# Windowed attention and a softplus MLP on one core: the written-out order of all work is replaced by another one

## The chip, the core and the metric

The kernel runs on one core of a Trainium2 chip. A core has five engines that each work through their own queue of instructions in order: TensorE (PE in the profile, with PEld for its weight loads), VectorE (DVE), ScalarE (ACT), GpSimd (POOL) and SyncE (SP), which here only issues DMA transfers. POOL and ACT issue DMA transfers too. [...]

The metric is the device time of one execution in microseconds. Before the change it is 343.13 us, the median of 3 runs (340.19 to 346.43).

## The reference: what is computed

Eight batches of eight heads, 576 positions, head size 64. Each position attends to the positions within 32 of its own and to 8 global positions; the 8 global positions attend to all. The result, laid out as 4,608 tokens of 512 features, goes through two matrix products with a softplus between them.

```python
scores = scale * np.matmul(q, k.transpose(0, 1, 3, 2))
mask = np.abs(pos[:, None] - pos[None, :]) <= window      # window = 32
mask = mask | is_global[:, None] | is_global[None, :]
scores = np.where(mask, scores, -1000000000.0)
scores = scores - np.max(scores, axis=-1, keepdims=True)
attn = np.exp(scores)
attn = attn / (np.sum(attn, axis=-1, keepdims=True) + 1e-09)
attn_out = np.matmul(attn, v)
x = attn_out.transpose(0, 2, 1, 3).reshape(B * S, H * D)  # 4608 x 512
h = x @ w_in                                              # 512 x 2048
g = np.maximum(h, 0.0) + np.log1p(np.exp(-np.abs(h)))
out = g @ w_out                                           # 2048 x 512
```

## The kernel before, in words

**Tiles.** The 4,608 tokens are nine tiles of 512 (m = 0 to 8). Attention works on groups of four blocks of 32 positions, called pairs in the code, n = 0 to 35, four to a tile, because 18 blocks make a batch and the tiles run across the batches. While TensorE works on the matrix products of tile m, the other engines prepare the attention of tile m + 1 (`AHEAD`, L409).

**One pair n from 4 on**, with the names that the profile gives: TensorE forms the scores (`sc`, L1040); VectorE adds the mask in two halves (`ma`, L1044) and takes the maximum (`mx`, L1057); GpSimd or VectorE subtracts it (`sub`, L1063); ScalarE takes the exponential (`ex`, L1080); VectorE sums and inverts (`su`, L1087 and L1089); GpSimd or VectorE multiplies by the inverse (`no`, L1095, output tile `pn`); VectorE transposes (`tp`, L1104, output tile `pt`). The first four pairs have the mask added by TensorE and go in halves (`mk` L1024, `mx` L1055, `ex` L1076). When the pairs of a tile (or of a piece of tiles 0 and 1) are there, TensorE multiplies by the values (`val`, L1207), and `xev` (L696, output tile `xT`) copies the result for the MLP.

**The global rows of batch b:** `sg` (L932), `mxg` (L942), `gexp` (L949), `tpg` (L954, L956, output tile `pgt`), `ov` (L965), `odd`, `both`, `gv` (L969 to L978). `pick` and `put` (L849, L862) fetch the keys and queries of the global positions; `fill` and `gev` copy them into place.

**Loads.** SP brings q, k and v of each batch as fp32 into three staging tiles (`load_part` L490 and L494 for q and k of batches 0 and 1, `load_qk` L440 for later batches, `load_v` L445). `cast` turns them into bf16 (L691 and L693 for q, L696 for k and v) on GpSimd, VectorE or ScalarE, and `turn` transposes (L789, L793; for batches 0 and 1 by TensorE, L820). A staging tile can be loaded again only after its cast. GpSimd issues the weights: `w_in` in four parts (L1304) and `w_out` in four parts (L1308), each cast from fp32 by the transfer. Two small transfers on SP, `follow` (L727), read the last bytes of `w_in` part 1 and of `w_out` part 1, so SP's later loads stay behind those weights. A one-column copy on GpSimd (L1385, `landed`) reads the end of one part of batch 1, so that `w_out` is issued only when this part is there; before the change it is `natural(0, 1)`, the q part for positions 256 to 511.

**The MLP.** `first` (L1242) is four matmuls for one of 16 slices of 128 hidden features, `soft` (L1248) is the softplus on ScalarE, `second` (L1253) one matmul of the second product, `oev` (L696, tile `osb`) the copy out of PSUM, and a store follows on GpSimd's queue for tiles 0 to 5 and on ScalarE's afterwards (L1265).

**The order.** All this work is 1,721 jobs, numbered as they are added (`_Order.add`). `ORDER` is a tuple of one number per job: five times the job's number plus its engine (0 PE, 1 ACT, 2 DVE, 3 POOL, 4 the loads on SP). It fixes which engine does each job and the sequence on every engine. `run` (L179) walks through `ORDER`, keeps a clock of its own from the costs given at `add`, and sorts the jobs by that clock before they are written out; no job of one engine passes another. So costs, `SLOW`, `NEED` and `STARVE` make no instruction: they shape the order where one is searched for, and here, with the order given, only how the five sequences are interleaved in the program text, and how many idle matmuls `keep` (L135) puts into TensorE's planned pauses before 34 us (`fill_in`, L701, the `warm` rows).

**The shared-port flags.** Jobs marked `port` (the casts, `sub`, `no`, `gv`, and after the change `make_own`) are treated in the clock of `run` as not able to run on VectorE while GpSimd computes (L217 to L220). [...]

Of the kernel before, what the change touches and what calls it, by code (L numbers as in the profile page):

```python
# [19 lines left out]
class _Order:  # L20
# [111 lines left out]
    FILL = 0.55  # L132
    fill = None

    def keep(self, t0, t1, order):  # L135
# [8 lines left out]
        count = int((t1 - t0) * self.FILL / 220)  # L144
        key = ("warm", len(order))
        j = dict(cost={"PE": (0, 0)}, emit=lambda e: self.fill(key, count), at=t0, end=t0 + count * 220, on="PE", n=-1, deps=[])
        self.fetch = self.stall(t0, count * 220, 2 * count)[1]
# [31 lines left out]
    def run(self, free):  # L179
# [13 lines left out]
        self.mine, self.other = 0, (0, 0)  # L193
        self.fetch, self.issued = (self.ASK, self.NEED, [], 0), 0
        while ready:
# [6 lines left out]
            for j in self.picked(ready):  # L202
# [57 lines left out]
            if e == "DVE" and j["port"]:  # L260
                self.mine = t + step
            if e == "POOL" and not j["moves"]:
                self.other = t, t + step
# [19 lines left out]
def kernel(  # L283
# [10 lines left out]
    nc = tc.nc  # L294
# [414 lines left out]
    def had(*keys):  # L709
        return [T[key] for key in keys]  # L710
# [715 lines left out]
```

## Time and profile before

| | before |
|---|---|
| time, median of 3 runs | 343.13 us (340.19 to 346.43) |
| profiled execution | span 340.5 us, 12,210 instructions; no other time of this execution is given |
| PE busy | 319.2 us (94%) |
| DVE busy | 259.4 us (76%) |
| ACT busy | 230.0 us (68%) |
| POOL busy | 169.1 us (50%) |
| DMA moved | 42.74 MB |
| first matmul of the MLP | 30.17 us after the start of the span |
| last matmul of attention values (`val` of tile 8) | 306.42 to 307.92 us |

How to read it: the profile is one execution. Busy times are sums over an engine's instructions, and a row of a group gives the operation, output and input tiles, the count, then the busy time and the mean of one. A row of the waits gives engine, line, what it waited for, and then the total in us, how often, and the longest. Rows of the timeline begin with the start in us from the start of the span and the duration. Queues of the DMA: q1 is SP's, q0 is GpSimd's.

### The profile page before, as it was taken

To read this page: it belongs to the slowest core of one execution; us is meant where nothing else is said; L and a number is where in the kernel's file an instruction comes from. 1 tells how busy PE (TensorE), PEld (TensorE's weight loads), DVE (VectorE), ACT (ScalarE), POOL (GpSimd) and SP (SyncE) were. 2 spreads that over 40 slices of the span, in tenths; PEclk is the share of its full clock that TensorE was granted. 3 is DMA by queue.
4 is the path that set the end of the run, shared out by engine and by line. 5 is a ranking of instruction groups with operands and counts; after the bars stand their busy time and mean duration, and the time that the engine had idled before them with its cause. 6 is when DMAs were issued, how large, how long until landed. Compare 5 with 4: busy or idle time off the path is not lost.

```text
span 340.5 us, 12210 instructions
## 1 busy us (share of the span) xinstructions
PE 319.2 (94%) x5333; PEld 169.4 (50%) x5333; DVE 259.4 (76%) x409; ACT 230.0 (68%) x469; POOL 169.1 (50%) x155
## 2 busy tenths in 40 slices
PE   6787899988999999999799999999999989999996
PEld 3435785555555454544354445444544444445443
DVE  7598679994999799979999999799985979061000
ACT  5688789975687866489638583769466746765442
POOL 5464457863695789608375328644532431460000
PEclk9679999999999999999999999999999999999999
DMA  7999499979799999999950997008111020002003
GB/s 193 220 173 244 123 162 191 175 142 192 127 171 211 174 204 185 189 151 231 164 132 34 173 165 177 2 2 171 36 56 39 33 97 2 31 31 96 0 0 123
DMA packets 168733, 42.74 MB, mean 126 GB/s; under 512 B 153192, under 2 KB 165736, under 8 KB 168680
## 3 DMA queue, kind: packets, MB, share of 16 engines
q1 hardware_dynamic: 160664, 28.33, 47.4%
q0 software_dynamic: 6144, 10.49, 13.2%
q10 hardware_dynamic: 1872, 3.15, 2.5%
q8 instruction: 41, 0.67, 0.9%
q14 instruction: 12, 0.10, 0.1%
HBM read 36.71 MB, written 9.44 MB: 136 GB/s over the span
## 4 chain that ended last, share of the span: by engine, by line
PE 41%; DVE 23%; SPq 11%; POOL 7%; DMA 7%; issue 6%; ACT 4%; POOLq 0%; DVEq 0%; ACTq 0%
PE h L1242 19%; PE o L1253 15%; SPq L440 7%; SPq L445 4%; DMA stage<-in_q_dram 4%; DVE sm L1087 4%; PE xo L1207 3%; POOL pn L1095 3%; DVE st L1044 2%; DMA stage<-in_v_dram 2%; POOL st L1063 2%; PE s L1040 2%; DVE gm L942 2%; DVE m L1057 2%; DVE pn L1095 2%
## 5 line engine op out<-in xcount | busy, mean ns | idle before, releaser
L1253 PE MATMUL o<-wout,g 128*128 128x512 bf16 (+1 forms) x592 | 137.4, 374 | 0.0
L1242 PE MATMUL h<-xT,win 128*128 128x512 bf16 (+3 forms) x768 | 135.8, 326 | 0.4 <-DVE xT L696 0.2
L1248 ACT ACTIVATE g<-h 128x512 bf16<-128x512 f32 (+3 forms) x192 | 85.5, 501 | 44.8 <-PE h L1242 43.7
L1242 PEld LDWEIGHTS <-win 128*128 128x128 bf16 x768 | 67.3, 98 | 60.3 <-issue 1.2
L1253 PEld LDWEIGHTS <-g 128*128 128x128 bf16 x592 | 55.3, 98 | 60.7 <-ACT g L1248 1.3
L1063 POOL TENSOR_TENSOR st<-st,m 128x1024 f32<-128x1024 f32 x27 | 51.9, 1931 | 49.4 <-DVE m L1057 49.3
L1095 POOL TENSOR_TENSOR pn<-st,rs 128x1024 bf16<-128x1024 f32 (+1 forms) x29 | 51.4, 1783 | 48.5 <-DVE rs L1089 46.4
L1044 DVE TENSOR_TENSOR st<-s,mask 128x512 f32<-128x512 f32 x64 | 41.5, 676 | 12.0 <-PE s L1040 12.0
L1087 DVE TENSOR_REDUCE sm<-st 128x8 f32<-128x1024 f32 x32 | 38.3, 1197 | 8.6 <-ACT st L1080 8.6
L1057 DVE TENSOR_REDUCE m<-st 128x8 f32<-128x1024 f32 x32 | 38.4, 1207 | 0.4
L1080 ACT ACTIVATE st<-st 128x1024 f32<-128x1024 f32 x32 | 32.9, 1057 | 1.1 <-POOL st L1063 1.0
L1104 DVE STREAM_TRANSPOSE pt<-pn 128x512 int32<-128x512 int32 x36 | 24.6, 690 | 3.9 <-POOL pn L1095 3.6
L696 ACT CAST xT<-xo 128x512 bf16<-128x512 f32 (+3 forms) x31 | 12.9, 476 | 17.9 <-PE xo L1207 17.9
L696 ACT COPY osb<-o 128x512 f32<-128x512 f32 (+1 forms) x29 | 16.6, 577 | 11.1 <-PE o L1253 9.8
L1095 DVE TENSOR_TENSOR pn<-st,rs 128x1024 bf16<-128x1024 f32 (+1 forms) x11 | 19.9, 1818 | 0.1
L696 POOL CAST kb<-stage 128x1152 bf16<-128x1152 f32 (+2 forms) x12 | 14.4, 1218 | 8.1 <-DVE rs L1089 5.1
L949 ACT ACTIVATE pg<-sg,gnb 128x320 bf16<-128x320 f32 (+1 forms) x32 | 14.9, 575 | 5.0 <-DVE gnb L943 5.0
L693 POOL TENSOR_SCALAR qb<-stage 128x1152 bf16<-128x1152 f32 (+2 forms) x10 | 12.9, 1286 | 10.7 <-DMA stage<-in_v_dram 7.3
L1248 ACT ACT_TABLE_LOAD x13 | 16.7, 1283 | 0.5 <-PE h L1242 0.3
L1040 PE MATMUL s<-kx,qx 64*32 64x128 bf16 x1152 | 15.4, 224 | 1.3 <-DVE qx L789 0.6
L696 POOL CAST vb<-stage 128x1152 bf16<-128x1152 f32 x11 | 12.6, 1145 | 7.2 <-DMA stage<-in_v_dram 5.5
L1265 POOL DMA_DIRECT2D out_dram<-osb x24 | 14.0, 584 | 3.7 <-DVE osb L696 3.7
(124 smaller groups left out, 313.2 us busy)
## 6 DMA issues: line engine op xcount, KB each, us to landing
stage<-in_v_dram SPq DMA_DIRECT2D x64, 144.0 KB, 4.6
stage<-in_k_dram SPq DMA_DIRECT2D x48, 144.0 KB, 3.8
stage<-in_q_dram SPq DMA_DIRECT2D x48, 144.0 KB, 3.6
out_dram<-osb POOLq DMA_DIRECT2D x24, 256.0 KB, 3.2
out_dram<-osb ACTq DMA_DIRECT2D x11, 256.0 KB, 2.1
stage<-in_k_dram SPq DMA_DIRECT2D x4, 512.0 KB, 9.1
stage<-in_q_dram SPq DMA_DIRECT2D x4, 512.0 KB, 6.2
win<-in_moe_w_in_dram POOLq DMA_DIRECT2D x4, 512.0 KB, 6.9
```

The source lines that it names most:

```text
L440: eng.dma_start(out=stage[w][quad(r), :, e, :], in_=SRC[w][b, HG * g:HG * g + HG].rearrange("a (c i e) (f d) -> e f i (a c) d", i=BL, e=2, ...
L696: {"ACT": nc.scalar.copy, "DVE": V.tensor_copy, "POOL": nc.gpsimd.tensor_copy}[e](out, in_)
L1044: V.tensor_tensor(out=PS["st", n][:, h, :, :], in0=PS["s", n, h][:, :, :], in1=mask[:, h, j0:j0 + PB, :, :].rearrange("p j s i -> p j (s i ...
L1057: V.reduce_max(out=m[:], in_=flat(PS["st", n], h0, h1), axis=AX)
L1063: on(e).tensor_tensor(out=t, in0=t, in1=over(PS["m", n, y][:], SL * BL), op=OP.subtract)
L1080: nc.scalar.activation(out=t, in_=t, func=AF.Exp)
L1087: V.reduce_sum(out=sm[:], in_=flat(PS["st", n], h0, h1), axis=AX)
L1095: on(e).tensor_tensor(out=PS["pn", n][:, :, :, h0:h1].rearrange("p x s h -> p h x s"), in0=PS["st", n][:, h0:h1], in1=PS["rs", n, y][:].re ...
L1104: V.transpose(out=bass.AP(base.tensor, base.offset, ap=[list(base.ap[0]), [2 * STEP, PB // 2], [STEP + BL // 2, 2], [1, SL * BL]]), in_=PS ...
L1242: nc.tensor.matmul(out=h[:, :], lhsT=w_in_t[c // 4][:, kd, c % 4 * P:(c % 4 + 1) * P], rhs=PS["xT", m][:, kd, lo:hi], start=(kd == 0), sto ...
L1248: nc.scalar.activation(out=PS["g", m, c][:, lo:hi], in_=PS[key][:, lo_of(c, hi - lo)], func=AF.Softplus)
L1253: nc.tensor.matmul(out=PS["o", m, ns, a][:, :], lhsT=PS["g", m, kf][:, ns * P:(ns + 1) * P], rhs=w_out_t[kf // 4][:, kf % 4, a:z], start=( ...
```

## The change: what it does

`ORDER` is replaced. Read back into names, the same 1,721 jobs stand in it. TensorE's sequence keeps its shape: counted in matrix-product time that stands ahead of it, no `val` moves by more than 1.8 us. The jobs that change engine, for the kinds where any does:

| job | before | after |
|---|---|---|
| `no`, n from 4 | POOL 24, DVE 8 | POOL 27, DVE 5 |
| `sub` | POOL 27, DVE 5 | POOL 27, DVE 5 (other pairs) |
| `cast` of v, all batches | POOL 11, DVE 5 | POOL 11, DVE 2, ACT 3 |
| `cast` of q, batches 2 to 7 | POOL 7, DVE 4, ACT 1 | POOL 7, DVE 3, ACT 2 |
| `cast` of k, batches 2 to 7 | POOL 8, DVE 1, ACT 3 | POOL 9, DVE 2, ACT 1 |
| `cast`, batches 0 and 1, q and k | POOL 7, DVE 5, ACT 8 | POOL 7, DVE 4, ACT 9 |
| `xev`, 512 wide | DVE 11, ACT 17 | DVE 14, ACT 14 |
| `xev`, 128 wide | DVE 2, ACT 10 | DVE 5, ACT 7 |
| `oev` | DVE 8, ACT 28 | DVE 10, ACT 26 |
| `turn`, batches 0 and 1 | DVE 9, ACT 11 | DVE 11, ACT 9 |
| `fill`, `gev`, `gv`, `odd`, copy of `pick` together | DVE 8, ACT 30 | DVE 13, ACT 25 |

Changes between the table of exponentials and that of softplus in ScalarE's sequence: 25 before, 23 after.

The order on SP's queue (`part` batch, 0 for q or 1 for k, part; `half` is v of four heads; `load` is q or k of a whole batch):

```
before: ... part 1 q 0, part 1 k 0, part 1 k 1, part 1 q 2, part 1 k 2, part 1 q 1, half 1 0, half 1 1, load 2 k, load 2 q ...
after:  ... part 1 k 0, part 1 k 2, part 1 q 0, part 1 k 1, part 1 q 1, part 1 q 2, half 1 1, half 1 0, load 2 k, load 2 q ...
before: ... load 5 k, half 4 1, half 4 0, load 5 q, load 6 k, half 5 0, half 5 1, load 6 q, load 7 k, load 7 q, half 6 1 ...
after:  ... load 5 q, load 5 k, half 4 0, half 4 1, load 6 k, load 6 q, half 5 1, half 5 0, load 7 q, half 6 0, load 7 k ...
```

The `follow` transfer that waits for `w_out` part 1 is written with `half 1 0`; in the new order `half 1 1` stands ahead of it.

GpSimd around `w_in` and `w_out`:

```
before: held, w_in 0, cast v, w_in 1, cast v, w_in 2, no 0.0, w_in 3 ...
after:  held, w_in 0, w_in 1, w_in 2, cast v, no 0.0, make_ends, w_in 3 ...
before: cast k, cast k, cast q, landed, w_out 0, blank, make_ends, w_out 1, w_out 2, w_out 3, sub 4 ...
after:  cast k, cast q, cast k, landed, w_out 0, w_out 1, cast q, w_out 2, sub 5, sub 4, w_out 3, sub 7 ...
```

VectorE and GpSimd in the attention of tile 4 (pairs 16 to 19), the written sequences (`*` marks a port job on VectorE):

```
before, DVE:  ... mx 17, cast k 5*, oev, ma 19, cast q 5*, sub 20*, mx 18, su 16, oev, ma 19, mx 19, no 16*, mxg 4 ...
before, POOL: ... sub 16, cast v 4, sub 18, store, store, cast q 5, sub 17, sub 19, no 18 ...
after, DVE:   ... mx 18, ma 19, ma 20, ma 20, mx 20, mx 21, sub 17*, ma 19, su 16, no 16*, tp 16, mx 19, turn k 5 ...
after, POOL:  ... sub 16, store, sub 20, cast q 5, sub 18, cast k 5, cast k 5, cast q 5, store, cast v 4, sub 19 ...
```

The first tile: VectorE does, ahead of `tp` of pair 0, in addition a cast of k, a copy for k, `fill`, a cast of v and both `mx` of pair 3, and no longer `su` of pair 2, a copy for q and `gv`; `gv` of batch 0 goes to ScalarE, behind three exponentials of pairs 3 and 2.

The rest of the diff, with the tuple cut:

```diff
-    NEED = 442
+    NEED = 448
     FETCH = 3900
-    SLOW = ((30000, 9300), (37000, 6500), (51000, 7300), (62000, 6500), (250000, 5600), (1e9, 4200))
+    SLOW = ((14000, 7300), (30000, 10600), (37000, 6600), (62000, 7000), (80000, 7300), (200000, 6500), (1e9, 5000))
...
-    FILL = 0.55
+    FILL, FILLT, NARROW, NFILL, NFILLT = 0.55, 220, 0, 0.8, 140
+    STARVE = 900
...
-        count = int((t1 - t0) * self.FILL / 220)
+        thin = t0 < self.NARROW
+        share, step = (self.NFILL, self.NFILLT) if thin else (self.FILL, self.FILLT)
+        count = int((t1 - t0) * share / step)
...
-                    elif e == "DVE" and j["port"] and self.other[0] <= t + 100:
-                        t = max(t, self.other[1])
-                    elif e == "POOL" and not j["moves"]:
-                        t = max(t, self.mine)
+                    elif e == "DVE" and j["port"]:
+                        if self.other[0] <= t + 100 and self.other[1] > t:
+                            t = self.other[1] + self.STARVE
+                    elif e == "POOL" and t < self.mine[1]:
+                        t = self.mine[1] + (self.STARVE if t < self.mine[0] else 0)
...
     ORDER = (
-        42, 107, 121, 126, 47, 52, 92, 116, 9, 236, 221, 225, 240, 87, 132, 137, 83, 14, 251, 255, 97, 143, 102, 268,
...
-    LATE = 300
+    LATE = 200
...
-        gate = [T["soft", b - 2, 9]] if w < 2 else []
...
-            cost["DVE"] = (1290, 1370)
+            cost["DVE"] = (760, 840)
...
-                                    rank=-1 if x else 0, hold=2000 if x else 0, moves=2750)
+                                    rank=-1 if x else 0, hold=2000 if x else 0, moves=2950)
...
-    setup("make_own", lambda e: make_own(), {"DVE": (380, 460)}, [T["make_first"], T["part", 0, 0, 1]], rank=2)
+    setup("make_own", lambda e: make_own(e), {"DVE": (380, 460), "POOL": (850, 900)}, [T["make_first"], T["part", 0, 0, 1]], rank=2, port=True)
...
-            T["landed"] = o.add(pool(100), lambda e: nc.gpsimd.tensor_copy(seen[:, 0, :], natural(0, 1)[:, 0, 0, 0, 0:1]), [T["part", 1, 0, FULL]], rank=0)
+            T["landed"] = o.add(pool(100), lambda e: nc.gpsimd.tensor_copy(seen[:, 0, :], natural(1, 1)[:, 0, 0, 0, 0:1]), [T["part", 1, 1, 1]], rank=0)
...
-                                      [T["landed"], T.get(("w_out", a - 1))], rank=-1, hold=2300 if a else 0, moves=3050)
+                                      [T["landed"], T.get(("w_out", a - 1))], rank=-1, hold=800 if a else 0, moves=3200)
```

`natural(1, 1)` is the k part for positions 256 to 511. `make_own` stays on VectorE in the new order, and `NARROW` is 0, so the narrow idle matmuls are never used.

More of the change, by code (lines that the diff above doesn't have):

```diff
@@ L143, in keep @@
         n = min(free)[1]
-        count = int((t1 - t0) * self.FILL / 220)
+        thin = t0 < self.NARROW
+        share, step = (self.NFILL, self.NFILLT) if thin else (self.FILL, self.FILLT)
+        count = int((t1 - t0) * share / step)
         key = ("warm", len(order))
-        j = dict(cost={"PE": (0, 0)}, emit=lambda e: self.fill(key, count), at=t0, end=t0 + count * 220, on="PE", n=-1, deps=[])
-        self.fetch = self.stall(t0, count * 220, 2 * count)[1]
+        j = dict(cost={"PE": (0, 0)}, emit=lambda e: self.fill(key, count, thin), at=t0, end=t0 + count * step, on="PE", n=-1, deps=[])
+        self.fetch = self.stall(t0, count * step, 2 * count)[1]
         self.issued += 2 * count
@@ L192, in run @@
         dma = []
-        self.mine, self.other = 0, (0, 0)
+        self.mine, self.other = (0, 0), (0, 0)
         self.fetch, self.issued = (self.ASK, self.NEED, [], 0), 0
@@ L260, in run @@
             if e == "DVE" and j["port"]:
-                self.mine = t + step
-            if e == "POOL" and not j["moves"]:
+                self.mine = t, t + step
+            if e == "POOL":
                 self.other = t, t + step
@@ L640, in make_ends, with make_own @@
                               mask[:, :, 0:2, :, :].rearrange("p h j s i -> p h (j s i)"))
-    def make_own():
-        V.tensor_tensor(out=own[:], in0=over(posM[:], NG).unsqueeze(3).to_broadcast([P, NJ, NG, 2]),
+    def make_own(e):
+        on(e).tensor_tensor(out=own[:], in0=over(posM[:], NG).unsqueeze(3).to_broadcast([P, NJ, NG, 2]),
                         in1=under(gf[:], NJ).unsqueeze(3).to_broadcast([P, NJ, NG, 2]), op=OP.is_equal)
@@ L699, with fill_in @@
     idle = pgt[:].rearrange("p m i h -> p (m i h)")
-    def fill_in(key, n):
+    def fill_in(key, n, thin):
         ps = psum(key, [P, 512], FP32)
+        w = P if thin else 4 * P
         for x in range(n):
-            nc.tensor.matmul(out=ps[:, :], lhsT=idle[:, 0:P], rhs=idle[:, 0:512], start=True, stop=True)
+            nc.tensor.matmul(out=ps[:, 0:w], lhsT=idle[:, 0:P], rhs=idle[:, 0:w], start=True, stop=True)
     if WARM:
@@ L737, in emit @@
                     load_v(nc.sync, b, h, range(R))
-                T["half", b, h] = o.add({"DMA": (2200 if b else 0, 0)}, emit, deps, rank=0, moves=2500 if b else 3100, late=LATE if b > 1 else 0)
+                T["half", b, h] = o.add({"DMA": (2200 if b else 0, 0)}, emit, deps, rank=0, moves=4000 if b else 2700 + 600 * h, late=LATE if b else 0)
             T["load", b, w] = T["half", b, 1]
@@ L741, in add_load @@
             T["load", b, w] = o.add({"DMA": (4400, 0)}, lambda e: load_qk(nc.sync, b, w, (0, 2, 1, 3)), deps, rank=0,
-                                    moves=9000 if w else 8000, late=LATE, behind=had(("load", b - 1, 2)) if b == EARLY else [])
+                                    moves=9200 if w else 8800, late=LATE, behind=had(("load", b - 1, 2)) if b == EARLY else [])
     def add_parts(b):
@@ L769, in add_cast @@
             cost = {"POOL": (1410, 1490), "ACT": (1380, 1480)}
-            cost["DVE"] = (1290, 1370)
+            cost["DVE"] = (760, 840)
             if b == 0:
                 cost = {"POOL": (1150, 1250), "DVE": (760, 850)}
-            T["cast", b, w].append(o.add(cost, emit, [T["half", b, h] if w == 2 else T["load", b, w]] + early + gate, rank=10 * phase_of(b) + 4 if b else 1.5 if w == 2 else 0, port=True))
+            T["cast", b, w].append(o.add(cost, emit, [T["half", b, h] if w == 2 else T["load", b, w]] + early, rank=10 * phase_of(b) + 4 if b else 1.5 if w == 2 else 0, port=True))
     def add_prep(b):
```

6 lines of the change are left out of this document (3 added, 3 removed), and 143 rows, old and new, of the table ORDER.

## The prediction

> **What bounds the kernel now.** I read the page's busy times and chain first, then the stretches of the span, then TensorE's own waits from 30 us on, because that is where the change can be paid.
>
> ```profile
> PE 319.2 (94%) x5333; PEld 169.4 (50%) x5333; DVE 259.4 (76%) x409; ACT 230.0 (68%) x469; POOL 169.1 (50%) x155
> ...
> PE 41%; DVE 23%; SPq 11%; POOL 7%; DMA 7%; issue 6%; ACT 4%; POOLq 0%; DVEq 0%; ACTq 0%
> ```
>
> ```profile
> 0.00:30.00 30.00, 21.67 (x397) 10.68 (x397) 22.55 (x68) 21.57 (x79) 17.56 (x40) 0.83 1.08 196
> 30.00:90.00 60.00, 55.34 (x1213) 38.77 (x1214) 48.24 (x80) 46.92 (x129) 35.25 (x33) 1.00 0.91 169
> 90.00:160.00 70.00, 70.00 (x1243) 35.00 (x1240) 63.91 (x94) 52.92 (x84) 47.27 (x37) 1.00 1.02 185
> 160.00:310.00 150.00, 144.77 (x2356) 71.30 (x2341) 124.73 (x171) 96.16 (x157) 68.98 (x47) 1.00 0.37 81
> ```
>
> ```profile
> PE xo L1207 <- DVE pt L1104: 3.4, 3, 1.6
> PE ov L965 <- DVE pgt L956: 2.7, 2, 2.0
> PE xo L1207 <- issue: 1.2, 1, 1.2
> PE pick L849 <- POOL qb L693: 1.0, 1, 1.0
> PE s L1040 <- DVE qx L789: 0.6, 1, 0.6
> ```
>
> The first fence says that TensorE is the bound and that 23% of the chain lies on VectorE all the same. The second (start and end, length, then PE, PEld, DVE, ACT, POOL busy, granted clock, DMA share, GB/s) says where: from 30 to 90 us TensorE is idle for 60 − 55.34 = 4.7 us, from 90 to 160 not at all, and from 160 to 310 for 5.2 us; after that it runs out its last tile. The change removes no matmul, so after 30 us at most 9.9 us can be won. The third fence names them: 3.4 + 2.7 + 0.6 = 6.7 us wait for VectorE, 1.0 for a cast that waits for a load, 1.2 us for nothing the profile shows.
>
> **VectorE and GpSimd.** The flagged operations of VectorE stretch when GpSimd computes.
>
> ```profile
> L1095 DVE TENSOR_TENSOR pn<-st,rs 128x1024 bf16<-128x1024 f32 x8 | 17.4, 2170 | 0.1
> L696 DVE CAST vb<-stage 128x1152 bf16<-128x1152 f32 x5 | 7.3, 1469 | 0.0
> L691 DVE TENSOR_SCALAR qb<-stage 128x1152 bf16<-128x1152 f32 x4 | 6.3, 1564 | 6.1 <-issue 3.6 <-DMA stage<-in_q_dram 2.5
> L696 POOL CAST vb<-stage 128x1152 bf16<-128x1152 f32 x11 | 12.6, 1145 | 7.2 <-DMA stage<-in_v_dram 5.5 <-PE xo L1207 1.6
> L1095 POOL TENSOR_TENSOR pn<-st,rs 128x1024 bf16<-128x1024 f32 x24 | 46.2, 1936 | 42.4 <-DVE rs L1089 40.4 <-DVE pt L1104 1.2 <-ACT g L1248 0.8
> ```
>
> ```profile
> 157.87 1.52 POOL L693 TENSOR_SCALAR qb<-stage 128x1152 bf16<-128x1152 f32 x1
> 158.50 5.75 DVE L1095 TENSOR_TENSOR pn<-st,rs 128x1024 bf16<-128x1024 f32 x1
> 159.28 3.79 POOL L1063 TENSOR_TENSOR st<-st,m 128x1024 f32<-128x1024 f32 x2
> ...
> 179.83 1.30 DVE L1095 TENSOR_TENSOR pn<-st,rs 128x1024 bf16<-128x1024 f32 x1
> ...
> 189.53 0.75 DVE L696 CAST vb<-stage 128x1152 bf16<-128x1152 f32 x1
> ...
> 80.68 0.81 DVE L691 TENSOR_SCALAR qb<-stage 128x1152 bf16<-128x1152 f32 x1 [3.56 <-issue]
> ```
>
> Alone these take 1.30, 0.75 and 0.81 us, so the excess is 8 × (2.17 − 1.30) + 5 × (1.47 − 0.75) + 4 × (1.56 − 0.81) = 13.6 us. One multiplication stands from 158.50 to 164.25 us while GpSimd runs three operations back to back until 163.07: the stall is 5.75 − 1.30 = 4.45 us, and behind it come the global rows of batch 4, and the 2.0 us wait of `ov` for `pgt`.
>
> [...]
>
> Now the new sequence. Jobs in these classes on VectorE fall from 8 + 5 + 4, with five `sub` and a cast of k 23, to 5 + 2 + 3, with five `sub` and two casts of k 17. In work without stalls that is 3 × 1.30 + 3 × 0.75 + 0.81 less and 0.80 more, so −6.2 us; but VectorE takes over copies: net 3 `xev` of 512 columns, 2 `oev` of the same size, and ten small ones.
>
> ```profile
> 18.35 0.72 DVE L696 COPY qx<-tr 128x512 bf16<-128x512 bf16 x1
> ...
> 244.94 0.69 DVE L696 CAST xT<-xo 128x512 bf16<-128x512 f32 x1
> ```
>
> That is 5 × 0.69 = 3.4 us, and ten of at most 0.72 us, most of them far smaller in elements, which I put at half of it, 3.6 us: VectorE's plain work stays as it is, within 1 us. What can go is the excess: all 13.6 us if the new sequence really keeps clear, 13.6 × 6/23 = 3.5 us if each job is hit as often as before. No instruction enforces the spacing, only the sequence and the data, so I take the middle, 8 us, less one place that speaks against it (below). GpSimd gets 3 `no` at 1.94 us and a cast, some 7 us on an engine that is 50% busy; ScalarE gives up copies, and in the third fence TensorE does not wait for it.
>
> What that is worth on TensorE: the 2.0 us at `ov` falls to 0.5 (same stage, another stall in place of this one); of the other 1.8 us at `xo` after 160 us, 0.7 at `ov` and 0.6 at `s`, together 3.1, a third, 1.1 us, since VectorE there has 17% of its time free already. The remaining 1.6 us at `xo` is tile 1.
>
> ```profile
> 49.26 3.75 POOL L1063 TENSOR_TENSOR st<-st,m 128x1024 f32<-128x1024 f32 x2 [3.57 <-DVE m L1057]
> ...
> 67.75 1.90 POOL L1095 TENSOR_TENSOR pn<-st,rs 128x1024 bf16<-128x1024 f32 x1
> ...
> 72.22 0.38 PE L1207 MATMUL xo<-pt,vg 32*64 32x384 bf16 x8 [1.63 <-DVE pt L1104]
> ```
>
> Today the `no` of pair 7 is on VectorE (it, too, stretched); in the new order it is GpSimd's, one operation of 1.94 us and one issue of `w_out` more in a queue that today runs from 49.26 to 69.65. In that time stand five `sub` at 1.93, three `no` and two casts of v at 1.15, 17.8 of 20.4 us, so 2.6 us are idle and can take the new work in. The queue then ends between 69.7 and 72.3, `tp` 0.7 later, against 72.2: −1.8 to +0.8, I take −0.7.
>
> **The loads and w_out.**
>
> ```profile
> 36.70 0.61 POOL L696 CAST kb<-stage 128x512 bf16<-128x512 f32 x1 [1.03 <-DMA stage<-in_k_dram]
> ...
> 41.02 0.23 POOL L1385 COPY seen<-stage 128x1 f32<-128x1 f32 x1 [3.33 <-DMA stage<-in_q_dram]
> ...
> 43.46 2.23 POOL L1308 DMA_DIRECT2D wout<-in_moe_w_out_dram  x3
> ```
>
> ```profile
> SPq L727 <- DMA wout<-in_moe_w_out_dram: 14.9, 1, 14.9
> ```
>
> GpSimd waits until 41.02 for the last q part; in the new order for a k part that today is cast at 36.70 (it goes out fourth instead of third, among six, so I take 37.5). Part 1 of `w_out` then goes out at about 37.5 + 0.2 + 0.8 = 38.5 instead of 43.46. SP stands 14.9 us for it, and after that come v of batch 1, k and q of batch 2.
>
> ```profile
> 52.16 7.51 SPq L445 DMA_DIRECT2D stage<-in_v_dram  x8
> ```
>
> So q of batch 2, whose cast begins at 80.7, comes 3.5 to 5 us sooner, and more if `half 1 1`, now ahead of the waiting transfer, uses the 14.9 us (half of 7.51 us). The 1.0 us of TensorE at `pick` goes, and so does VectorE's 3.56 us of idle before its row at 80.68. What is late next there is VectorE itself, which TensorE does not feel between 90 and 160. Moved with the two `w_out` issues: the next cast of q on GpSimd's queue waits 0.8 us more behind them; it has to wait for its load anyway.
>
> While GpSimd's transfers run, SP's get nothing. From 19 to 28 us the DMA moved this:
>
> ```profile
> q0 software_dynamic: 1669, 1.66, 119.2%
> ...
> stage<-in_k_dram SPq DMA_DIRECT2D x2, 512.0 KB, 9.1
> ```
>
> and nothing on q1, though two loads of k were issued in these 9 us. [...] By the row the q part still on its way waits for all of `w_out`, which is a danger of this change.
>
> **The head, 0 to 30 us.**
>
> ```profile
> 27.39 1.49 issue
> ...
> 30.17 3.73 PE h L1242 x64
> ```
>
> The MLP starts at 30.17 after 1.49 us in which TensorE waited for nothing shown. `w_in` parts 1 and 2 go out with no cast between, pair 0 gets its exponentials first, but VectorE does some more before `tp` 0 (it is idle for 30 − 22.55 = 7.4 us of this stretch) and `gv` 0 stands behind three exponentials on ScalarE. The change of the idle matmuls' number follows the clock of the plan, which no row shows. Between −1.5 (that pause goes) and +1.5 (it doubles) I take 0.
>
> **The sum**, against the span of 340.5: −1.0 (`pick`) − 1.5 (`ov`) − 0.7 (tile 1) − 1.1 (the rest) + 1.0 = 337.2. The last term is for new waits: the sequence is fixed by a clock that errs, and the five waits quoted are 1 to 3 us each in today's order, so one of them anew is the least to expect. The profiled execution lies at the fast end of the three runs; the median is 343.13/340.5 = 1.008 times it, so 337.2 becomes 339.8.
>
> **Rivals.**
> (1) *All of it is won.* VectorE keeps clear and the loads come sooner: 6.7 + 1.0 us of waits and 1.5 us of the head go, no new wait comes: 331.3, as a median 333.9. For it: the waits hang together, the 4.45 us stall and the late load feed several of them. Against: six fewer flagged jobs of 23 only.
> (2) *The waits move.* What is taken from VectorE's stalls comes back as waits for GpSimd's 7 us more or for VectorE's copies; 340.5, 343.1. For it: plain work on VectorE is unchanged; 91% of 90 to 160 us is VectorE's, which leaves it no room to be clear of anything.
> (3) *Slower: GpSimd's runs hold VectorE longer.* In tile 4 the new GpSimd queue is `sub` 20, cast, `sub` 18, three casts. With the rows
>
> ```profile
> L1063 POOL TENSOR_TENSOR st<-st,m 128x1024 f32<-128x1024 f32 x27 | 51.9, 1931 | 49.4 <-DVE m L1057 49.3
> L696 POOL CAST kb<-stage 128x1152 bf16<-128x1152 f32 x8 | 12.1, 1549 | 5.1 <-DVE rs L1089 5.1
> L1057 DVE TENSOR_REDUCE m<-st 128x8 f32<-128x1024 f32 x32 | 38.4, 1207 | 0.4
> ```
>
> that is 2 × 1.93 + 4 × 1.55 = 10.1 us in one run, if q and k of batch 5 have landed; sooner loads make that likelier. `sub` 17 on VectorE comes up one `mx` (1.2 us) into it and would wait 8.9 us, against 4.45 us of stall and 2.5 us of waiting for a load in this stage today. TensorE then waits 2.0 + 1.9 = 3.9 instead of 0.5 at `ov`, and with the same again at the three casts of batch 6 ahead of `no` 19 (4.7 us of run) 3.6 more: 337.2 + 7.0 = 344.2, a median of 346.8. It decides from the point where GpSimd does not pause in that run. [...]
> (4) *Slower: q of batch 1 behind w_out.* If part 1 of q has not landed when the first `w_out` packets come (about 39.5), it waits for four parts of 0.5 MB at 1.66 MB in 9 us, 11 us.
>
> ```profile
> 50.02 0.65 ACT qx L696
> ```
>
> Its transpose is copied at 50.0 today; it would be at 39.5 + 11 + 2 for its own 0.5 MB + 2 for cast and transpose = 54.5, and TensorE, whose queue has the transpose in it, stands 4.5 us: 341.7, a median of 344.3.
>
> **How the numbers follow.** The forecast, 339.8, has 0.38; (1) 0.28; (2) 0.17; (3) 0.12; (4) 0.05. Two per cent, about what a measurement of this kernel tells from no change, is 336.3 below and 350.0 above. Faster by that: most of (1) and the low edge of the forecast, 0.23 + 0.07 = 0.30. Slower: (3) with a further stall of its kind, 0.07, and 0.04 for (2) and (4) with the spread of the runs: 0.11. Within: 0.59. The range takes in (1)'s 333.9 and (3)'s 346.8 with little to spare: 333 to 347.
>
> **What would show it.** `w_out` part 1 issued before 40 us and q of batch 2 cast before 78 us (loads); `pn`, `vb` and `qb` rows of VectorE at means near 1.3, 0.75 and 0.81 us (clear), or a row of over 6 us in tile 4 (rival 3); the wait of `ov` for `pgt` under 1 us; TensorE's idle between 160 and 310 us under 4 us; first matmul of the MLP between 28.7 and 31.7. The prediction is wrong if TensorE's waits after 30 us rise above 9.9 us, or if its matmuls themselves take another time.

## The result

The changed kernel takes 338.33 us, the median of 20 runs (336.54 to 343.19), beside 342.49 us for 20 runs of the kernel before (340.19 to 346.43). The ratio is 0.9891, with a 95% interval of 0.9869 to 0.9913: about 1.1% faster, which a measurement by 2% calls the same. The ratio is taken over the fast runs alone, so it is not the quotient of the two medians. A second comparison gave 338.08 beside 341.40 us, 0.9923 (0.9888 to 0.9957).

The busy times and the chain that ended last, of the page after:

```profile
PE 316.2 (94%) x5286; PEld 170.0 (51%) x5333; DVE 250.0 (74%) x416; ACT 224.2 (67%) x456; POOL 179.1 (53%) x159
...
PE 61%; DVE 9%; SPq 8%; DMA 8%; POOL 6%; issue 5%; ACT 1%; DVEq 0%; POOLq 0%
```

The same stretches as before (start and end, length, PE, PEld, DVE, ACT, POOL busy, granted clock, DMA share, GB/s):

```profile
0.00:30.00 30.00, 21.24 (x345) 10.24 (x349) 22.66 (x66) 19.84 (x75) 16.63 (x39) 0.72 1.12 208
30.00:90.00 60.00, 55.88 (x1255) 39.33 (x1266) 47.99 (x87) 43.99 (x126) 36.91 (x35) 1.00 1.01 181
90.00:160.00 70.00, 68.22 (x1215) 34.51 (x1227) 67.10 (x98) 49.93 (x78) 49.72 (x33) 1.00 0.76 142
160.00:310.00 150.00, 147.49 (x2363) 73.98 (x2382) 112.26 (x169) 100.75 (x160) 75.88 (x54) 1.00 0.43 96
```

And TensorE's waits from 30 us on:

```profile
PE o L1257 <- issue: 3.3, 21, 0.2
PE xo L1211 <- DVE pt L1108: 0.9, 2, 0.7
PE o L1257 <- DMA wout<-in_moe_w_out_dram: 0.8, 1, 0.8
PE h L1246 <- issue: 0.5, 3, 0.2
PE h L1246 <- DVE xT L700: 0.4, 2, 0.2
```

VectorE's share of the chain fell from 23% to 9%, TensorE's rose from 41% to 61%. The first row of the waits is none: this trace has 5,333 weight loads but 5,286 matmuls, and 21 gaps of at most 0.2 us stand where a record is missing. Without it the waits come to 4.0 us with the small ones that are not shown, against 9.5 us before. That is the gain: `ov` and `pick` are gone from the list, `xo` waits 0.9 instead of 3.4 us for `pt`. The head gave a little back: the first MLP matmul starts at 31.02 us instead of 30.17. The granted clock of the first 30 us is 0.72 instead of 0.83: in every trace with the new head it is halved for 17.1 us ahead of 31.2 us, in those with the old head for 10.2 us, and in three of these for 3.4 us more around 30 us. How much of the 0.85 us comes from this isn't shown.

```profile
31.02 2.19 PE L1246 MATMUL h<-xT,win 128*128 128x128 bf16 x34
```

From there to the end of the span it is 336.5 − 31.02 = 305.5 us, against 340.5 − 30.17 = 310.3 before: −4.8 us behind the head, +0.85 in it, −4.0 in all.

The flagged operations of VectorE after:

```profile
L1099 DVE TENSOR_TENSOR pn<-st,rs 128x1024 bf16<-128x1024 f32 x5 | 8.6, 1716 | 0.1
L1067 DVE TENSOR_TENSOR st<-st,m 128x1024 f32<-128x1024 f32 x5 | 6.9, 1390 | 0.0
L695 DVE TENSOR_SCALAR qb<-stage 128x1152 bf16<-128x1152 f32 x3 | 3.8, 1268 | 2.7 <-DMA stage<-in_q_dram 2.7
L700 DVE CAST kb<-stage 128x1152 bf16<-128x1152 f32 x2 | 2.6, 1292 | 0.2 <-issue 0.2
L700 DVE CAST vb<-stage 128x1152 bf16<-128x1152 f32 x2 | 1.8, 877 | 0.0
```

Against 1.30, 1.21, 0.81, 0.80 and 0.75 us alone the excess is 2.1 + 0.9 + 1.4 + 1.0 + 0.25 = 5.6 us, from 13.6. No row is longer than 2.4 us; before, one was 5.75 and one 4.35 us.

### The profile page after: what moved, and what is told of

Same layout as the page of the kernel before. It is cut to its first block, busy times and chain, and to the rows that moved or that the text cites. A ratio compares the mean times of both kernels' runs of the same rounds, so it can differ in the third digit from the quotient of the medians.

```text
span 336.5 us, 12158 instructions
## 1 busy us (share of the span) xinstructions
PE 316.2 (94%) x5286; PEld 170.0 (51%) x5333; DVE 250.0 (74%) x416; ACT 224.2 (67%) x456; POOL 179.1 (53%) x159
## 4 chain that ended last, share of the span: by engine, by line
PE 61%; DVE 9%; SPq 8%; DMA 8%; POOL 6%; issue 5%; ACT 1%; DVEq 0%; POOLq 0%
PE h L1246 26%; PE o L1257 24%; SPq L444 6%; PE xo L1211 3%; PE s L1044 3%; DMA wout<-in_moe_w_out_dram 3%; POOL pn L1099 2%; DMA stage<-in_q_dram 2%; DMA stage<-in_k_dram 2%; DVE st L1048 2%; DVE m L1061 1%; PE ov L969 1%; DMA stage<-in_v_dram 1%; POOL qb L697 1%; PE warm L709 1%
## 5 line engine op out<-in xcount | busy, mean ns | idle before, releaser
L1246 PE MATMUL h<-xT,win 128*128 128x512 bf16 (+3 forms) x758 | 132.5, 325 | 1.9 <-issue 0.5
L1257 PE MATMUL o<-wout,g 128*128 128x512 bf16 (+1 forms) x560 | 128.3, 373 | 4.7 <-issue 3.3
L1252 ACT ACTIVATE g<-h 128x512 bf16<-128x512 f32 (+3 forms) x192 | 84.3, 500 | 42.2 <-PE h L1246 40.7
L1099 POOL TENSOR_TENSOR pn<-st,rs 128x1024 bf16<-128x1024 f32 (+1 forms) x32 | 56.7, 1776 | 33.0 <-DVE rs L1093 27.3
L700 ACT COPY osb<-o 128x512 f32<-128x512 f32 (+1 forms) x27 | 15.3, 571 | 20.1 <-PE o L1257 15.1
L700 DVE CAST xT<-xo 128x512 bf16<-128x512 f32 (+3 forms) x23 | 12.1, 564 | 13.6 <-PE xo L1211 13.4
L700 ACT CAST xT<-xo 128x512 bf16<-128x512 f32 (+3 forms) x25 | 10.6, 474 | 16.3 <-PE xo L1211 16.1
L697 POOL TENSOR_SCALAR qb<-stage 128x1152 bf16<-128x1152 f32 (+1 forms) x11 | 14.5, 1315 | 9.3 <-DMA stage<-in_q_dram 6.6
L700 POOL CAST kb<-stage 128x1152 bf16<-128x1152 f32 (+1 forms) x12 | 17.2, 1455 | 3.0 <-DMA stage<-in_k_dram 3.0
L1044 PEld LDWEIGHTS <-qx 64*32 64x32 bf16 x1152 | 10.9, 94 | 13.3 <-issue 8.9
```

Source lines behind the costliest of these rows:

```text
L700: {"ACT": nc.scalar.copy, "DVE": V.tensor_copy, "POOL": nc.gpsimd.tensor_copy}[e](out, in_)
L1044: nc.tensor.matmul(out=PS["s", n, g][quad(a ^ g), x, :], lhsT=qx[b % 2][rows(g), a, j * BL:(j + 1) * BL], rhs=kx[b % 2][rows(g), a, e0 * B ...
L1099: on(e).tensor_tensor(out=PS["pn", n][:, :, :, h0:h1].rearrange("p x s h -> p h x s"), in0=PS["st", n][:, h0:h1], in1=PS["rs", n, y][:].re ...
L1246: nc.tensor.matmul(out=h[:, :], lhsT=w_in_t[c // 4][:, kd, c % 4 * P:(c % 4 + 1) * P], rhs=PS["xT", m][:, kd, lo:hi], start=(kd == 0), sto ...
L1252: nc.scalar.activation(out=PS["g", m, c][:, lo:hi], in_=PS[key][:, lo_of(c, hi - lo)], func=AF.Softplus)
L1257: nc.tensor.matmul(out=PS["o", m, ns, a][:, :], lhsT=PS["g", m, kf][:, ns * P:(ns + 1) * P], rhs=w_out_t[kf // 4][:, kf % 4, a:z], start=( ...
```

## Experiments: where the gain is

Theory A is the prediction's: VectorE's stalls make TensorE wait, most of all from tile 4 on, and what VectorE no longer loses there is the gain. Theory B: VectorE has slack, and the sooner weights and loads made it. Theory C: what is taken from VectorE comes back through GpSimd's longer runs.

**Give VectorE its lost time back.** Thirteen reductions are put behind three jobs of the changed kernel.

```diff
+    PAD = {771: 6, 1241: 5, 1421: 2}
     for job in o.run(...):
         job["emit"](job["on"])
+        for x in range(PAD.get(job["n"], 0)):
+            V.reduce_max(out=padm[:], in_=pos[:, :], axis=AX)
```

> The changed kernel with 13 more reductions of 128x576 on VectorE, whose result nothing uses: six behind the pn of tile 4, five behind the q cast near 180 us, two behind the sub near 255 us. By size between the 128x320 and 128x1024 reductions of the trace they take some 0.65 us each, 8.5 us in all, about what the change saved on VectorE's port operations. Theory A (from tile 4 on VectorE sets the pace, so the 8 us it no longer loses are what the change gained): the time rises by 4 to 8.5 us, to 342.3 to 346.8. Theory B (VectorE has slack there, 86 us of the span in all, and the gain came from the weights and from waits that went elsewhere): at most 1 us, 338.3 to 339.3.

Measured: 345.57 us, 1.0138 times the kernel before (1.0089 to 1.0188), so 7 us above the changed kernel. That lies in A's interval and not in B's. TensorE's longest waits show where it was paid, and the stretch from 171.1 us (columns as above) what came on top:

```profile
PE pick L866 <- ACT picked L700: 2.6, 1, 2.6
PE h L1246 <- DVE st L1048: 1.6, 1, 1.6
PE ov L969 <- DVE pgt L960: 1.2, 1, 1.2
```

```profile
171.10:174.50 3.40, 3.40 (x35) 1.27 (x19) 3.30 (x8) 2.35 (x6) 2.52 (x2) 0.50 1.09 174
```

The thirteen took 0.75 us each, 9.7 us in all. The six in tile 4 (4.5 us) came out at `pick` and `ov` almost in full (3.8 us), the five at 180 us at `h` (1.6 of 3.8 us). And behind the pauses of 2.6 and 1.2 us the granted clock is 0.50 for 3.4 us, by an estimate from that clock 3.4 × 0.50 = 1.7 us more. Here TensorE's pauses cost more than their length. This shows that VectorE's time at these places reaches TensorE; whether the change gained there is for the next runs.

**Take VectorE's six worst losses out of the kernel before.** In `ORDER` a job on VectorE has 5n + 2, on GpSimd 5n + 3; nothing else is edited, no position changes.

```diff
-1917  -3857  -5587  -6207  -7047  -7257
+1918  +3858  +5588  +6208  +7048  +7258
```

> The kernel before, with its sequence kept and only the six VectorE operations that lost most to GpSimd (at 68, 158, 183, 190, 225 and 273 us; 19.9 us on VectorE) handed to GpSimd at the same place of the sequence, where they cost some 10 us. Theory A: the time falls by 2 to 5 us, to 337.5 to 340.5. Theory B: within 1 us of 342.5. Third theory C (GpSimd's longer runs then hold tp and the scores as long as the stalls did): 342.5 to 346.

Measured: 342.15 us, 1.0036 (1.0005 to 1.0068): nothing won, as C has it. But the trace shows that the swaps behind tile 4 did what A says (`ov` is gone from the waits) and one of the six cost everything:

```profile
PE xo L1207 <- DVE pt L1104: 6.3, 3, 4.6
```

```profile
75.80:79.20 3.40, 3.40 (x99) 2.28 (x85) 3.13 (x6) 2.13 (x9) 1.48 (x1) 0.50 1.23 213
```

The `no` of pair 7 (1917), the last of its piece of tile 1, now stands behind GpSimd's other work; TensorE waits 4.6 us for its transpose, and the clock is halved behind it. (`pick` and the wait of `s` for VectorE are gone too, but not by the swaps: in the next run, where TensorE isn't held at tile 1, they are back with 0.8 and 0.5 us.) So the next run leaves that one on VectorE.

```diff
-3857  -5587  -6207  -7047  -7257
+3858  +5588  +6208  +7048  +7258
```

> The kernel before with five of the six operations handed to GpSimd in place; the pn of tile 1 (68 us) stays on VectorE, because handing that one over opened a pause of 4.66 us on TensorE ahead of the values of tile 1, behind which the granted clock was 0.5 for 3.4 us (1.7 us more). Theory A (idle of TensorE ends the time, and the stalls of VectorE behind tile 4 make some 4 us of it): 337.5 to 339.5. Theory C (GpSimd's longer runs give all back): 341.5 to 343.

Measured: 337.75 us, 0.9895 (0.9874 to 0.9916). Five changed numbers of 1,721 give the kernel before all that the change gave. In TensorE's waits the 2.7 us at `ov` are gone and 0.6 of the 1.2 us at `xo` without a releaser; the 3.3 us at `xo` for `pt`, 0.8 at `pick` and 0.5 at `s` stay. One job more or less is 4.4 us. This does not show that the change owes its gain to the same five (in its order three of them are still on VectorE and two on ScalarE). It does show that the place of a stall counts and not the sum: by the same groups of rows this kernel's VectorE still loses 9.4 us, 6.1 of it in one cast

```profile
183.35 6.88 DVE L696 CAST vb<-stage 128x1152 bf16<-128x1152 f32 x1
```

for which nobody waits.

**Halves of the two orders.** EARLY are the jobs that the order named first plans to start before 160 us.

```diff
+ORDER = [x for x in FIRST if x // 5 in EARLY] + [x for x in THEN if x // 5 not in EARLY]
```

> The new sequence for all work planned to start before 160 us, then the old sequence for what is left; code and constants are those of the changed kernel. Theory A (the gain lies behind tile 4): 341 to 343. Theory B (it lies in the head and the first tiles): 338 to 339.5.

> The old sequence for all work planned to start before 160 us, then the new one for what is left; code and constants are those of the changed kernel. Theory A: 337.5 to 340. Theory B: 341.5 to 343.

Measured: new, then old: 341.83 us, 1.0025 (0.9987 to 1.0063). Old, then new: 339.22 us, 0.9943 (0.9910 to 0.9976). The new head, with its sooner weights and loads, is worth nothing alone, the new tail about half of the gain, within A's interval; B's intervals hold in neither. What stands out in the trace of "old, then new" (an execution of 341.2 us, 2 us above the median) is tile 1: GpSimd's store was issued there at 68.4 instead of 69.6 us, just ahead of VectorE's `pn` instead of behind it, and

```profile
68.57 4.38 DVE L1099 TENSOR_TENSOR pn<-st,rs 128x1024 bf16<-128x1024 f32 x1
```

(2.67 us in the kernel before) held the values of tile 1 for 3.4 us. That this is the missing half was argued only; mending it did not bring it (below).

**The weights.** `landed` reads the last q part again, and it and the first three parts of `w_out` stand behind that part's load.

```diff
-            T["landed"] = o.add(pool(100), lambda e: nc.gpsimd.tensor_copy(seen[:, 0, :], natural(1, 1)[:, 0, 0, 0, 0:1]), [T["part", 1, 1, 1]], rank=0)
+            T["landed"] = o.add(pool(100), lambda e: nc.gpsimd.tensor_copy(seen[:, 0, :], natural(0, 1)[:, 0, 0, 0, 0:1]), [T["part", 1, 0, FULL]], rank=0)
```

> The changed kernel with w_out put back: its first three parts wait for the last part of batch 1's q again, as before. If sooner w_out is worth time, o waits for w_out at about 54 to 62 us by 2 to 4 us and the time is 340.5 to 342.5. If it is not, the other loads of batch 1 come sooner by as much and the time is 337.8 to 339.

Measured: 338.28 us, 0.9936 (0.9906 to 0.9966), the time of the changed kernel. The parts 0 to 2 of `w_out` went out at 39.2 to 40.7 us, against 37.1 to 39.5 in the changed kernel and 41.2 to 44.2 in the kernel before, because the q part itself comes sooner in the new order of the loads. So this run undoes 1 to 2 us of 4 to 6, and that much of `w_out` is worth nothing that these intervals can tell. For the rest there are "new, then old" above, where the sooner weights gave nothing, and the five swaps, which gave the gain without them.

```diff
 GpSimd's queue:
  w_out part 2
+ w_out part 3
  sub
  sub
- w_out part 3
  sub
  sub
```

> The changed kernel with w_out's last part issued directly behind the third, ahead of four sub on GpSimd instead of between them. Theory: the 1.0 us that o waits for this part at 61.9 us goes, and nothing else is late by it: 0.7 to 1.1 us below the changed kernel, 337.3 by the first comparison. Rival: the part then takes the DMA engines from the v halves and the last parts of batch 1, so that ov or pick wait instead: no gain, or up to 1 us more.

Measured: 339.67 us, 0.9972 (0.9939 to 1.0004). The wait of `o` for `w_out` is gone, as expected, but the time is not lower. In the profiled execution the loss is a pause at 274.0 us, far from the edit, for which the profile names no releaser, and the halved clock behind it:

```profile
PE xo L1211 <- issue: 2.0, 1, 2.0
```

```profile
276.40:279.80 3.40, 3.40 (x59) 1.51 (x54) 3.12 (x5) 2.36 (x3) 0.00 (x0) 0.50 0.02 5
```

The runs of this kernel lie between 337.5 and 343.0 us. What makes this pause, and whether the edit makes it likelier, stays open.

## Experiments: when VectorE loses to a whole run of GpSimd

The traces had both: flagged operations that got in after one GpSimd operation (2.51 us for a `pn` at 273.14 in the kernel before), and some that waited for three to five (5.75 us at 158.50 there, 6.88 us in the run of the five swaps). Theory L: VectorE always gets in when the GpSimd operation in progress ends. Theory R: it waits for the end of the run. The first probe has only these operations.

> No part of the computation, only the two engines' order: 54 trials in which GpSimd has four to six operations one behind the other (sub 128x1024, some with casts 128x1152) and VectorE first a reduction of 0.35 to 3.7 us and then one flagged operation (pn, sub or a cast of 128x1024) that waits for nothing but the port. Theory L (one operation at a time: VectorE enters when the GpSimd operation in progress ends): the flagged operation lasts at most 1.9 us above its own 1.2 us (0.7 us for the cast), whatever the offset, and the next GpSimd operation is 1.2 us longer. Theory R (VectorE waits for the end of the run, as at 158.50 us before): it lasts its own time and the rest of the run, some 7 us at the smallest offset and 4 us at the largest. If both occur, which of them an offset or a kind of operation decides is read from the trials.

It was theory L in all 54 trials. The first two rows are GpSimd's, the last VectorE's:

```profile
28.70 1.90 POOL L56 TENSOR_TENSOR t<-t,go 128x1024 f32<-128x1024 f32 x1 [0.31 <-ACT go L74]
...
30.55 2.87 POOL L56 TENSOR_TENSOR t<-t,go 128x1024 f32<-128x1024 f32 x1
...
29.97 1.70 DVE L66 TENSOR_TENSOR xb<-x,go 128x1024 bf16<-128x1024 f32 x1
```

VectorE starts at 29.97 in the middle of the first `sub`, gets in when that ends at 30.60, and the second `sub`, already started, lasts 2.87 instead of 1.90 us (behind a cast on VectorE it is lengthened by 0.44 us only). With eight offsets, in us from the start of the trial:

```
start of VectorE's pn     1.14  1.55  1.97  2.28  2.70  3.22  3.64  4.05
its length                2.12  1.70  1.28  2.83  2.41  1.89  1.47  2.91
its end                   3.26  3.25  3.25  5.11  5.11  5.11  5.11  6.96
end of the sub under way  2.18  2.18  2.18  4.03  4.03  4.03  4.03  5.89
```

What then did the long stalls have in common? In every trace here they met a run that GpSimd had opened with the issue of a store, as this one, on GpSimd, around the cast of 6.88 us above:

```profile
181.28 0.59 POOL L1265 DMA_DIRECT2D out_dram<-osb  x1 [3.71 <-DVE osb L696]
181.90 1.91 POOL L1063 TENSOR_TENSOR st<-st,m 128x1024 f32<-128x1024 f32 x1
183.74 1.50 POOL L696 CAST kb<-stage 128x1152 bf16<-128x1152 f32 x1
185.14 1.16 POOL L696 CAST vb<-stage 128x1152 bf16<-128x1152 f32 x1
186.24 1.91 POOL L1063 TENSOR_TENSOR st<-st,m 128x1024 f32<-128x1024 f32 x1
188.11 1.50 POOL L693 TENSOR_SCALAR qb<-stage 128x1152 bf16<-128x1152 f32 x1
189.49 0.85 POOL L1265 DMA_DIRECT2D out_dram<-osb  x1
```

VectorE's cast comes up at 183.35 and gets in at about 189.5, with the next issue. That is theory D, and the second probe adds the store.

> As the first probe, no part of the computation: 24 trials in which GpSimd also issues a store, as it does between the operations of the kernel. Six runs of GpSimd (D: issue of a store, s: sub, c: cast) by four offsets of VectorE's flagged operation: Dssss with pn and with a cast, sDsss, sssDs, DDcsss, DsDss. In the kernels each flagged operation that lost to more than one GpSimd operation (158.50, 183.41 before) met a run that GpSimd had opened with the issue of a store, and got in at the run's end or at the next issue; those that met a run without one got in after one operation, as in all 54 trials of the first probe. Theory D (behind an issue GpSimd keeps the port until it idles or issues again): 1.2 us and the rest of the run, up to 7 us in Dssss, and at most 1.9 us more than its own in the stretch of a run that lies before its issue. Theory L (the issue has nothing to do with it): at most 1.9 us more in all of them.

```profile
20.49 0.57 POOL L53 DMA_DIRECT2D out_dram<-o  x1
21.08 7.45 POOL L61 TENSOR_TENSOR t<-t,go 128x1024 f32<-128x1024 f32 x4
...
21.54 8.08 DVE L71 TENSOR_TENSOR xb<-x,go 128x1024 bf16<-128x1024 f32 x1
```

The same four `sub` as in the first probe, behind one issue: now none of them is stretched (4 take 7.45 us), and VectorE ends at 29.62, 1.1 us behind the run. Length in us of the flagged operation by run and offset (D issue, s `sub`, c cast):

```
           first    second   third    fourth offset
Dssss pn   1.22     8.08     7.45     6.30
Dssss cast 8.27     7.46     6.83     5.69
sDsss      2.59     1.94     1.32     6.31   (the fourth starts behind the issue)
sssDs      2.67     1.94     1.32     2.02   (all start ahead of it)
DDcsss     1.22     6.17     5.55     4.41
DsDss      3.40     2.63     2.01     5.13   (three get in with the second issue)
```

Of 24 trials, 15 start behind an issue, and all of them wait for the end of the run or for the next issue; 7 start ahead of it and lose at most one operation; 2, with 1.22 us, get in at once: one starts 0.02 us into the issue, the other 0.22 us into the first of two. The first of DsDss starts 0.22 us into its issue as well and waits, so what decides in that first moment stays open. Theory D holds for all that start later, and L and R are both right, each for its kind of run. In the kernels of this case it holds too: from 45 us on, every flagged operation of q, k, v, `sub` and `no` that came up at least 0.2 us behind the start of the last issue, with more of GpSimd's run to come than the operation under way, got in at the end of that run (5.75 us at 158.50 and 4.35 us at 183.41 before, 6.88 us with the five swaps). In the first probe no operation lost more than 1.7 us, in the second operations of 1.2 us took up to 8.08 us. Why the issue has this effect, no run here shows.

Back in the kernel, two runs on the order "old, then new". First, a GpSimd copy of one column that reads VectorE's `pn` ahead of the store's issue at 68 us, so that GpSimd waits and not VectorE:

```diff
+    o.add(pool(100), lambda e: nc.gpsimd.tensor_copy(seen[:, 1, :], PS["pn", 7][:, 0, 0:1, 0]), had(("no", 7, 0)), rank=0, uses=[("pn", 7)])
```

> The kernel of the old sequence up to 160 us and the new one behind it, with one thing more: at 68 us a GpSimd copy of one column reads the pn of tile 1 that VectorE makes, ahead of the store's issue and the two kb casts, so that GpSimd waits for VectorE's pn instead of VectorE for GpSimd's run. There pn took 4.38 us, TensorE then stood 3.46 us ahead of the values of tile 1, and the granted clock was 0.5 for 3.4 us behind that. Theory A: pn takes at most 2.2 us, TensorE's pause is under 1 us, the clock stays 1.00, and the time falls by 3 to 5 us from 339.2, to 334.2 to 336.2. Rival: the kb casts, now some 1.3 us later, hold the scores of the next tile: no gain, 338.5 to 340.

Measured: 340.69 us, 0.9959 (0.9921 to 0.9997). The place itself is mended,

```profile
69.60 1.48 DVE L1099 TENSOR_TENSOR pn<-st,rs 128x1024 bf16<-128x1024 f32 x1
```

TensorE waits for `pt` by 0.7 us at most instead of 3.4, and no halved clock follows there. But TensorE now reaches tile 4 sooner, and the stall of 5.7 us at 158 us, which in "old, then new" cost it nothing, is felt:

```profile
PE ov L969 <- DVE pgt L960: 2.3, 1, 2.3
```

```profile
169.50:172.90 3.40, 3.29 (x8) 1.22 (x8) 3.37 (x5) 1.56 (x5) 0.31 (x1) 0.50 1.04 208
```

One stall hid another. Second, no store is issued by GpSimd at all:

```diff
-                o.add({"POOL": (700, 2700)}, lambda e, ns=ns: store(nc.gpsimd, ns, 0, d_model), [T["oev", m, ns]], ...
+                o.add({"POOL": (700, 2700)}, lambda e, ns=ns: store(nc.scalar, ns, 0, d_model), [T["oev", m, ns]], ...
```

> The kernel of the old sequence up to 160 us and the new one behind it, with one edit: the 24 stores that GpSimd issues are issued by ScalarE at the same places, where one takes 0.34 us as the later stores show (8 us of ScalarE in all, which is busy for 231 of 340 us). No GpSimd run behind 45 us then begins with an issue. Theory D: no flagged operation of VectorE loses more than one GpSimd operation any more: the pn at 68 us takes at most 3.1 us (4.38 there, and without the copy that held GpSimd), the one at 158 us at most 3.1 us (5.78), TensorE's pause ahead of the values of tile 1 is under 1.8 us and the granted clock stays 1.00 behind it; 334.5 to 337. Theory L (the issue is not the reason): the two stay at 4.4 and 5.8 us and the time at 338.5 to 340. Rival: the issues on ScalarE hold softplus and exp, and the time is 339.5 to 342 although the two are short.

The flagged operations did what theory D says: the `pn` at 68 us takes 1.50 us, the one of 5.78 us takes 2.75,

```profile
166.06 2.75 DVE L1099 TENSOR_TENSOR pn<-st,rs 128x1024 bf16<-128x1024 f32 x1
```

and the excess of the flagged groups is 2.1 us, against 9.4 in "old, then new". But the time is 360.07 us, 1.0561 (1.0508 to 1.0615), which neither theory nor the rival foresaw. SP's loads now wait for stores by the profile,

```profile
SPq L444 <- DMA out_dram<-osb: 55.2, 10, 14.1
SPq L449 <- DMA out_dram<-osb: 13.8, 5, 5.5
```

so q of two batches comes late, and TensorE waits 4.6 us at `pick` and 9.5 us at `h`. In the other orders of this kernel no load waits for a store. Why they do when ScalarE issues the stores wasn't tried; a layout that keeps stores off GpSimd without this would be the next thing to try. None of these kernels is faster than the changed one by more than its interval.

## Why the prediction was right, point by point

**The time.** 339.8 was forecast, 338.33 measured; the forecast's own case came.

**What bounds the kernel** held: at most 9.9 us behind 30 us could be won, and 4.8 were, all of them TensorE's waits. That VectorE's share of the chain is real was the right reading: with 9.7 us more of it the time rose by 7.

**The terms.** `pick`, forecast at −1.0, went. `ov` and "the rest", −1.5 − 1.1 (a third of 3.1 is 1.0), and tile 1, −0.7, were too small: 2.7 us of `ov`, 2.5 of the 3.4 us at `xo` and 0.3 us of `s` are gone, −5.5 instead of −3.3, and 1.2 us of `xo` without a releaser went as well. The term of new waits, +1.0, was too small too: 0.8 us for the last part of `w_out`, 1.3 us at `h` where there were 0.4, and some small ones make 2.2 (0.5 of it, at `h` without a releaser, may be missing records as at `o`). By these waits the sum is −1.0 − 5.5 − 1.2 + 2.2 = −5.5, by the span behind the head −4.8. The head, taken at 0 with ±1.5, cost 0.85. So −3.3 was forecast and −4.0 came. That they are so near is in part luck: waits that went beyond the forecast by 3.4 us met new waits and a head that were 2.1 us more than forecast.

**VectorE's excess** was forecast to fall by 8 us, and it fell by 8.0. Its plain work "stays as it is, within 1 us": busy time fell by 9.4 us, so the rest by 1.4; two set-up operations of the head are 2.0 us shorter (`own` 0.45 instead of 1.42 us, `ident` 0.27 instead of 1.32), and without them the reading holds. But the sum was the wrong measure: the five swaps leave 9.4 us of excess and are worth as much as the whole change.

**The step that failed** is the reading of the row at 158.50 by which rival (3) has `sub` 17 wait for the end of GpSimd's run. One row was taken for a rule. Behind a store's issue, as at 158.50, the second probe has it too (up to 8.08 us for 1.2); in the first probe, whose runs have no issue, no operation lost more than 1.7 us. So rival (3), the new run of tile 4 that was to hold `sub` 17 for 8.9 us, did not come: that run begins behind 6.3 us in which GpSimd was idle, not behind an issue; `sub` 17 took 2.08 us, and the q cast behind it on GpSimd was stretched instead.

```profile
150.18 2.08 DVE L1067 TENSOR_TENSOR st<-st,m 128x1024 f32<-128x1024 f32 x1
...
151.16 2.44 POOL L697 TENSOR_SCALAR qb<-stage 128x1152 bf16<-128x1152 f32 x1
```

The new order's clock does not tell the two kinds of run apart either: it only starts VectorE's flagged work 0.9 us (`STARVE`) behind whatever GpSimd does, store or none. That no flagged operation of the new order meets a run with a store at its head for long is seen in its trace (none lasts over 2.4 us), not in its plan; its `sub` at 186.26 us comes up 0.04 us into an issue with a GpSimd `sub` and a `no` behind it and gets in at once (1.22 us), which is luck as far as the plan goes.

**The loads.** `w_out` part 1 was to go out at 38.5 us; two parts went out from 37.08 on. The q of batch 2 was to come 3.5 to 5 us sooner, and its loads were all issued by 71.6 us instead of 76.6. Of its two casts, GpSimd's began at 75.00 us instead of 80.82. VectorE's, which the forecast quotes, began at 79.65 instead of 80.68 and missed the 78 us of the list; but VectorE no longer idles 3.56 us ahead of it, it is busy with other work, as the forecast has it.

```profile
37.08 1.58 POOL L1312 DMA_DIRECT2D wout<-in_moe_w_out_dram  x2
...
55.44 0.79 POOL L1312 DMA_DIRECT2D wout<-in_moe_w_out_dram  x1
...
63.78 7.79 SPq L444 DMA_DIRECT2D stage<-in_q_dram  x8
...
75.00 1.48 POOL L697 TENSOR_SCALAR qb<-stage 128x1152 bf16<-128x1152 f32 x1
...
79.65 1.57 DVE L695 TENSOR_SCALAR qb<-stage 128x1152 bf16<-128x1152 f32 x1
```

So the wait at `pick` went as forecast: the later cast now ends at 81.22 us, before it ended at 82.85, and TensorE comes to this product at 82.9. The step of this part that failed is that k of batch 2 takes its time of before: its eight loads now meet the last part of `w_out`, issued at 55.44.

```profile
51.60 12.07 SPq L444 DMA_DIRECT2D stage<-in_k_dram  x8
```

Before the change they took 6.50 us, but began 8.2 us later, so q was not late by it. "SP's get nothing" was too hard: while that part moves, SP's queue gets a quarter of all bytes (from 57 to 61 us; packets, MB, share):

```profile
q0 software_dynamic: 459, 0.46, 86.7%
q1 hardware_dynamic: 1204, 0.15, 25.8%
```

Rival (4), q of batch 1 behind `w_out`, would be a wait of TensorE for it; none of these passes 0.3 us.

## What to carry to other kernels

Find which engine's time reaches the bound before counting stalls: a stall of 6.1 us cost nothing, 4.5 us of work in another tile cost 3.8 us and a halved clock behind it. Moving single jobs of a fixed order is a cheap test of it, one job at a time, since one of six hid what the other five had won. And where VectorE's operations wait for GpSimd's as in these runs, keep them away from GpSimd runs that begin with a store's issue: in the probes an operation of 1.2 us took up to 8.08 us behind one, and none lost more than 1.7 us in runs without one. Letting GpSimd wait for VectorE's result before the issue mended one such place here, but not the time.

## What the runs showed of the hardware that was not expected

After an issue of a store by GpSimd, VectorE's `pn` and casts (and one `sub`, 4.20 us in "new, then old") waited in these runs for the end of GpSimd's run or its next issue: operations of 1.2 and 0.7 us took up to 8.08 and 8.27 us in the probe. Without it they lost at most the rest of the one operation under way (1.7 us in the probe), and the GpSimd operation behind it was up to 1.0 us longer (2.87 instead of 1.90 us in the probe).

A pause of TensorE was often followed by a granted clock of 0.50 for 3.4 us, which by the estimate above costs 1.7 us: behind pauses of 4.6, 3.4, 2.3 and 2.0 us and two of 2.6 and 1.2 us close together here, not behind the 2.0 us at `ov` in the kernel before. The length of the pause does not decide alone: with `landed` put back, the clock was halved from 44.4 to 47.8 us though no pause ahead of it passed 0.73 us; in the 3.5 us before, TensorE was busy for 2.27 us.
